# First stage of a two-stage transform: from one 90-frequency product per part to a 60-frequency and a 30-frequency product, with the second stage one step later

## The chip, the cores and the metric

The kernel runs on one core of one Trainium2 chip. The metric is device time in microseconds (us) of one launch; lower is better. Before the change, three runs gave 921.55, 926.01 and 921.55 us, median 921.55 us. The profiled execution took 916.37 us, of which 914.5 us lie between the first and the last instruction (the span). Shares and durations below are of that span.

## The reference

The reference is a long convolution followed by a soft mixture of experts. All is float32.

```python
# x: (8, 5696, 128), h: (5696, 128)
Y = irfft(rfft(x, 2*S, axis=1) * rfft(h, 2*S, axis=0), 2*S, axis=1)[:, :S, :]
# the result, as 45568 tokens of 128 channels, goes through soft MoE
logits = Y @ phi                       # 32 slots
slot_input = softmax_over_tokens(logits).T @ Y
slot_out[e] = relu(slot_input[e] @ w1[e]) @ w2[e]   # 8 experts, 4 slots each
out = softmax_over_slots(logits) @ slot_out
```

## The kernel before

The convolution is a transform, a product of spectra and a transform back. A sequence of 5696 = 89 x 64 tokens is seen as 89 rows of 64 columns, and 5760 = 90 x 64 frequencies are computed: one of each conjugate pair of an 11520-point transform, so that real tables suffice. The work goes in three parts that run at the same time, each some steps behind the one ahead of it.

**Part A, the first stage** (`stage_a`, L205 to L220). It works on chunks: 9 groups (the filter h and the 8 batches) times 8 chunks make 72. A chunk is 4 columns and the 4 mirrored ones, loaded by `load_x` (L179) into one of 3 buffers `xc`, on partitions 20 to 108. `fold` (L196, GpSimd) makes from them the sum (comp 0) and the difference (comp 1), 128 x 512 each, in `x0` and `x1`. `stage_a(c, comp)` then multiplies the folded rows by two of three tables: 90 frequencies, in two runs of 45 that stand at columns F0 = 6 and F1 = 82 of a stationary operand of 128 columns. Each product fills one PSUM bank (128 x 512); ScalarE copies it into `fst`, and two DMAs of 45 rows write the result to an HBM scratch `f` of the group. A chunk thus costs 4 products, 4 evictions and 4 DMAs.

**Part B, the second stage** (`load_g`, `stage_b1`, `stage_b2`, L230 to L302). It works on units: 12 for each group, 11 of 4 pairs of frequencies and a last one of 1. A unit is loaded from `f` (`gt`, 3 buffers, two units ahead), multiplied on TensorE in 64 x 64 pieces (L250), multiplied by the filter's spectrum on VectorE (L268, L277), transformed back by the second stage of the inverse (L292), evicted by ScalarE (L297) and written to a scratch `z`. Since a unit needs all chunks of its group, B runs behind A by LAG_B steps.

**Part C** (`load_pair`, `stage_c1` to `stage_c6`). It works on 32 pairs of chunks, one for every two steps: load from `z` (`zc`), inverse of the first stage (L347), unfolding (VectorE L352, L353, GpSimd L366), transposes (L375), logits (L384), softmax pieces and the slot sums (L460). It runs LAG_C steps behind A.

After the last step a tail finishes C, runs the experts (L762 to L792) and writes the output (L817 to L834).

**What sets the order.** The program order is written out by hand: one loop over steps t (L561), in which each engine's instructions are queued in the order of the calls. Step t holds chunk t of A, 1 or 2 units of B in turn (`PER`), and half of a pair of C. Every engine works through its own queue in that order. Nearly all DMAs are issued by SyncE (SP), also in order: a DMA that has to wait for its data holds up those behind it in SP's queue. The lags are

```python
LAG_B, LAG_C = NJ + 1, 3 * NJ + 3      # 9 and 27 (NJ = 8)
```

A is at two places of a step: `stage_a(t, 0)` and `fold(t + 1, 0)` first (L589), `stage_a(t, 1)` and `fold(t + 1, 1)` late (L630). Between them lie B's first slot, C's products or transposes, B's second slot, and the loads for later steps. `prefetch` (L568) issues a unit's load as soon as its group has been through A by program order (`queue[loaded][0] // NW * NJ + NJ <= t`); the DMA itself waits for the writes of `f`. `bank()` hands out 4 PSUM banks in a ring, which A and C share. `fst` has 5 buffers.

The loop has 81 steps: 9 with A alone, 8 with A and the filter's B, 10 with A and the first batch units, 45 with A, B and C, and 9 with B and C alone.

Of the kernel before, what the change touches and what calls it, by code (L numbers as in the profile page):

```python
# [10 lines left out]
F32 = mybir.dt.float32  # L11
# [8 lines left out]
    return [(0, 64, 32), (64, n - 64, 0)]  # L20


def transform_tables(S, N1, N2, CH, X0, F0, F1):

    N, R1, HALF, P = N1 * N2, S // N2, N2 // 2, 2 * N2
    k1 = np.arange(N1)
    alpha = np.pi * (k1 + 0.5) / N1
    m1 = np.arange(R1) - (N1 - 1) / 2
    a1 = np.outer(m1, alpha)  # L40
    s1 = np.stack([np.cos(a1), -np.sin(a1), -np.cos(a1)], 1)
    a0 = np.outer(alpha, np.arange(N1 // 2) + 0.5)
    i1 = np.stack([np.cos(a0), -np.sin(a0), -np.cos(a0)], 1)
    NP = N1 // 2
    part = s1
    s1 = np.zeros((P, 3, P))
    for a, p in enumerate((F0, F1)):
        s1[X0:X0 + R1, :, p:p + NP] = part[:, :, a * NP:(a + 1) * NP]
    part = i1[np.arange(N1).reshape(2, NP).T.reshape(-1)]
    i1 = np.zeros((P, 3, N2))  # L50
    for r, n, p in z_blocks(N1):
        i1[p:p + n, :, 0:NP] = part[r:r + n]
    k2 = np.arange(N2)
    omega = np.pi * (k1[:, None] + 2 * N1 * k2[None] + 0.5) / N
    m2 = np.arange(HALF) - (N2 - 1) / 2
    a2 = m2[None, :, None] * omega[:, None, :]
    w = np.concatenate([np.cos(a2), np.sin(a2)], 1)
    back = np.arange(N2).reshape(2, HALF // CH, CH).transpose(1, 0, 2).reshape(-1)
# [12 lines left out]
    return [np.ascontiguousarray(t, dtype=np.float32) for t in (s1, i1, wq, vq, tn)]  # L71
# [3 lines left out]
def kernel(  # L75
# [24 lines left out]
    nc = tc.nc  # L100
    P = 128
    B, S, D = x.shape
    NSL = moe_phi.shape[1]
    E, _, F = moe_w1.shape
    SPE = NSL // E
    NFC = F // P
    N1, N2 = 90, 64
    R1, HALF, NP = S // N2, N2 // 2, N1 // 2
    CH = 4
    NJ = HALF // CH  # L110
# [5 lines left out]
    HP = P // 2  # L116
    NQ = NJ // 2
    assert S == R1 * N2 and R1 == N1 - 1 and D == P and CH == Q == 4
    SPLIT = R1 // 16 * 16
    X0, F0, F1 = 20, 6, 82  # L120
    ctx.enter_context(tc.manual_schedule())

    t_s1, t_i1, t_w, t_v, t_turn = [
        nc.inline_tensor(t, f"tab_{n}").ap()
        for n, t in zip(("s1", "i1", "w", "v", "turn"), transform_tables(S, N1, N2, CH, X0, F0, F1))]
    fd = [nc.dram_tensor(f"f_{g}", (2, N2, NP, 2, D), F32, kind="Internal").ap() for g in range(B + 1)]
    zd = [nc.dram_tensor(f"z_{b}", (NP, 2 * N2, 2, D), F32, kind="Internal").ap() for b in range(B)]
    cd = nc.dram_tensor("c_t", (P, B * NQ, Q, 2, MH), F32, kind="Internal").ap()
# [7 lines left out]
    i1 = const.tile([P, 3, HP], F32, name="i1")  # L136
# [21 lines left out]
    apool = lead.enter_context(tc.tile_pool(name="apool", bufs=2, side="right"))  # L158
    bpool = front.enter_context(tc.tile_pool(name="bpool", bufs=1))

    s1 = apool.tile([P, 3, P], F32, name="s1", tag="s1", bufs=1)
    wt = fconst.tile([P, NP, HP], F32, name="wt")
    vt = fconst.tile([P, NU, 2, HP], F32, name="vt")
    turn = fconst.tile([P, 2, NW, 2, 2], F32, name="turn")
# [6 lines left out]


    xs = {}
    xf = [apool.tile([P, CH, D], F32, name=f"x{i}", tag=f"x{i}", bufs=1) for i in range(2)]
    xcs = [apool.tile([P, 2, CH, D], F32, name=f"xc{i}", tag=f"xc{i}", bufs=1) for i in range(3)]
    for t_ in xcs:
        nc.vector.memset(t_[:, :, :, :], 0.0)
# [16 lines left out]
    folded = {}  # L194

    def fold(c, comp):  # L196
        if c not in xs:
            return
        t_ = xs.pop(c) if comp else xs[c]
        y_ = xf[comp]  # L200
        nc.gpsimd.tensor_tensor(out=y_[:, :, :], in0=t_[:, 0, :, :], in1=t_[:, 1, ::-1, :],  # L201
                                op=AL.subtract if comp else AL.add)
        folded[(c, comp)] = y_

    def stage_a(c, comp):  # L205
        g, j = divmod(c, NJ)
        src = folded.pop((c, comp))
        tab = (0, 1) if comp == 0 else (1, 2)
        st = apool.tile([P, CH, 2, D], F32, name="fst", tag="fst", bufs=5)
        for G in range(2):  # L210
            p = bank()
            nc.tensor.matmul(p[:, :], s1[:, tab[G], :],  # L212
                             src[:, :, :].rearrange("p n d -> p (n d)"), start=True, stop=True)
            nc.scalar.activation(st[:, :, G, :],  # L214
                                 p[:, :].rearrange("p (n d) -> p n d", d=D), AF.Copy)
        n0 = comp * HALF + CH * j
        for a, p in enumerate((F0, F1)):
            nc.sync.dma_start(
                out=fd[g][a, n0:n0 + CH, :, :, :].rearrange("n q c d -> q n (c d)"),
                in_=st[p:p + NP, :, :, :].rearrange("k n c d -> k n (c d)"))  # L220


    gs, prods = {}, {}

# [303 lines left out]
        tail["once"] = once  # L528


    LAG_B, LAG_C = NJ + 1, 3 * NJ + 3
    PER = [1, 2] * (NJ // 2)
    assert sum(PER) == NW
    NA, NC = (B + 1) * NJ, B * NJ
# [26 lines left out]
    for t in range(last_front + 1):  # L561
        us = list(units(t))

        def pair(lag):
            T, half = divmod(t - LAG_C - lag, 2)
            return T if half == 0 and 0 <= T < NT else None

        def prefetch(last):  # L568
            nonlocal loaded
            while loaded < len(queue) and queue[loaded][0] <= last \  # L570
                    and queue[loaded][0] // NW * NJ + NJ <= t:
                load_g(queue[loaded][0])
                loaded += 1

        turns = {2: (1, 3), 1: (2,)}.get(len(us), ())

        def slot_b(place=None):
            if place is not None and place not in turns:
                return
            fresh = bool(us)  # L580
            if fresh:
                u = us.pop(0)
                prefetch(u + AHEAD)
                stage_b1(u, t < LAG_C or t >= NA)
                wait_b2.append(u)
            if len(wait_b2) > fresh:
                stage_b2(wait_b2.pop(0))

        if t < NA:  # L589
            stage_a(t, 0)  # L590
            fold(t + 1, 0)
        if pair(3) is not None:
            dispatch(pair(3))
        if t < last_front:
            slot_b(1)
        T, U = pair(0), pair(2)
# [12 lines left out]
        rows = (lambda: None) if U is None else (lambda: stage_c4(U))  # L609
        after = None  # L610
        if T is not None:
            after = stage_c1(T, rows)
        else:
            rows()
        if pair(1) is not None:
            stage_c2(pair(1))
        if pair(5) is not None:
            stage_c6(pair(5))
        if after:
            after()  # L620
        slot_b(2)
        if pair(-2) is not None:
            load_pair(pair(-2))
        if t < NA:
            load_x(t + 3)
        if t == NJ:
            prefetch(AHEAD)
        if U is not None:
            stage_c5(U)
        if t < NA:  # L630
            stage_a(t, 1)
            fold(t + 1, 1)
        if pair(1) is not None:
            stage_c3(pair(1))
        slot_b(3)
        if pair(1) is not None:
            column_max(pair(1))
        if U is not None:
            softmax(U)
        if t == NA:  # L640
            lead.close()
            wts = inner.enter_context(tc.tile_pool(name="wts", bufs=1, side="right"))
            w1s = wts.tile([P, E, F], F32, name="w1s")
        if NA < t <= NA + E:
            nc.sync.dma_start(out=w1s[:, t - NA - 1, :], in_=moe_w1[t - NA - 1])


# [10 lines left out]
                      in_=zring[0][gap, :, :, :, :, :].rearrange("k h o n c d -> k (h o n c d)"))  # L658
# [7 lines left out]
    y_ = tail["pool"].tile([P, Q * CH, D + 1], F32, name="y2", tag="y2", bufs=1)  # L666
# [27 lines left out]
    for V in range(T, NT):  # L694
# [169 lines left out]
```

## Time and profile before

| what | value |
|---|---|
| median time | 921.55 us |
| span of the profile | 914.5 us |
| busy: TensorE, VectorE, ScalarE, GpSimd | 89%, 71%, 53%, 44% |
| bytes moved by DMA, mean rate | 272.43 MB, 298 GB/s |
| time of DMA packets on the SP queue | 91.7% of 16 DMA engines' span |
| first-stage products (L212) | 576 records, 273.9 us |
| first-stage evictions (L214) | 288, 171.8 us |
| folds (L201) | 144, 183.1 us |
| writes of `f` (L218) | 288 DMAs of 180 KB |

A matmul of float32 leaves two records in the profile, so 576 records are 288 products. Busy time of TensorE is that of overlapping, pipelined instructions; the chain of waits (what released what, followed back from the end) tells better how long a product holds up the next one. The share of DMA is the time that packets took on the 16 DMA engines; since packets overlap a little, it can pass 1.00 where the engines always have work.

### The profile page before, as it was taken

What the parts mean: (1) busy time and instruction counts of PE and PEld (TensorE: products, weight loads), DVE (VectorE), ACT (ScalarE), POOL (GpSimd) and SP (SyncE); (2) the same over time, 40 slices, a digit from 0 to 9 for tenths busy, and PEclk for the clock granted to TensorE, in tenths of its full rate; (3) what the DMA queues carried; (4) which work ended last, traced back from release to release, by engine and by line L of the source; (5) the groups of instructions that cost most, each with busy time, mean ns of one, the idle gap of its engine ahead of it and who ended that gap; (6) DMA issues with size and microseconds to landing.
All of it is one profiled execution on the core that took longest, in us unless ns stands there. A gap on an engine that the chain in (4) does not pass through costs nothing.

```text
span 914.5 us, 19226 instructions
## 1 busy us (share of the span) xinstructions
PE 812.2 (89%) x7220; PEld 425.9 (47%) x7220; DVE 645.8 (71%) x928; ACT 481.1 (53%) x888; POOL 405.2 (44%) x385
## 2 busy tenths in 40 slices
PE   6968888799999999999999999999988776978893
PEld 2323344344454444544555445444444443345783
DVE  3058767667888878877888777868888885774552
ACT  4624445456556565655666565555654344474442
POOL 4624333245555555555555555555533432472000
PEclk9989999999999999999999999999999998788865
DMA  9999899999999999999999999989989998751798
GB/s 302 269 282 310 256 326 347 292 323 340 285 324 331 304 281 323 320 329 280 329 323 317 289 317 313 311 281 325 334 266 338 305 295 206 223 220 74 281 404 340
DMA packets 156550, 272.43 MB, mean 298 GB/s; under 512 B 11766, under 2 KB 114422, under 8 KB 153317
## 3 DMA queue, kind: packets, MB, share of 16 engines
q1 hardware_dynamic: 155883, 270.85, 91.7%
q8 instruction: 58, 0.95, 0.4%
q10 hardware_dynamic: 576, 0.36, 0.2%
q14 instruction: 33, 0.27, 0.1%
HBM read 142.86 MB, written 128.21 MB: 296 GB/s over the span
## 4 chain that ended last, share of the span: by engine, by line
PE 61%; DMA 27%; issue 4%; ACT 2%; DVE 2%; POOL 2%; SPq 1%; DVEq 0%; POOLq 0%; ACTq 0%
PE bank L212 19%; PE bank L347 10%; PE bt L250 9%; DMA zc<-z 8%; PE bz L292 7%; DMA gt<-f 6%; DMA out_dram<-o 4%; PE bank L375 3%; PE bank L460 3%; DMA zd<-z 3%; DMA z<-zst 2%; DMA f<-fst 2%; PE bank L384 2%; PE bank L436 2%; PE op L817 1%
## 5 line engine op out<-in xcount | busy, mean ns | idle before, releaser
L201 POOL TENSOR_TENSOR x<-xc 128x512 f32<-128x512 f32 x144 | 183.1, 1273 | 260.5 <-PE bank L212 156.9
L212 PE MATMUL bank<-x,s 128*128 128x512 f32 x576 | 273.9, 611 | 9.7 <-POOL x L201 9.6
L214 ACT ACTIVATE fst<-bank 128x512 f32<-128x512 f32 x288 | 171.8, 597 | 94.7 <-PE bank L212 88.3
L297 ACT ACTIVATE zst<-bz 128x1024 f32<-128x1024 f32 x96 | 93.2, 971 | 195.2 <-PE bz L292 191.5
L268 DVE TENSOR_TENSOR p<-bt,Hi 128x1024 f32<-128x1024 f32 x96 | 113.0, 1177 | 107.3 <-PE bt L250 107.1
L212 PEld LDWEIGHTS bank<-x,s 128*128 128x128 f32 x576 | 102.1, 192 | 126.9 <-issue 94.1
L250 PE MATMUL bt<-gt,wt 64*64 64x256 f32 x1620 | 117.4, 397 | 40.0 <-DMA gt<-f 19.8
L347 PE MATMUL bank<-zc,i 128*64 128x512 f32 x480 | 118.0, 614 | 8.5 <-DMA zc<-z 6.2
L277 DVE TENSOR_TENSOR yf<-bt,p 128x512 f32<-128x512 f32 x192 | 119.4, 663 | 3.3
L268 DVE TENSOR_TENSOR bt<-bt,Hr 128x1024 f32<-128x1024 f32 x96 | 113.0, 1178 | 0.0
L250 PEld LDWEIGHTS bt<-gt,wt 64*64 64x64 f32 x1620 | 55.9, 134 | 117.0 <-issue 61.7
L292 PE MATMUL bz<-yf,vt 64*64 64x256 f32 x1440 | 103.7, 386 | 0.0
L366 POOL TENSOR_TENSOR y<-y,op 128x512 f32<-128x512 f32 x64 | 77.4, 1209 | 11.8 <-DVE op L352 9.1
L292 PEld LDWEIGHTS bz<-yf,vt 64*64 64x64 f32 x1440 | 61.8, 136 | 21.1
L366 POOL TENSOR_TENSOR y<-y,om 128x512 f32<-128x512 f32 x54 | 64.0, 1185 | 2.1
L347 PEld LDWEIGHTS bank<-zc,i 128*64 128x64 f32 x480 | 30.9, 138 | 70.3 <-issue 47.4
L375 PE MATMUL bank<-ident,y 109*128 109x109 f32 x512 | 57.5, 268 | 0.7 <-DVE y L366 0.7
L375 PEld LDWEIGHTS bank<-ident,y 109*128 109x128 f32 x512 | 51.2, 146 | 12.9 <-POOL L L449 6.2
L421 POOL MEMSET dt<- 64x8 f32 x32 | 3.4, 106 | 115.9 <-issue 69.2
L377 ACT ACTIVATE yt<-bank 128x360 f32<-128x360 f32 x128 | 50.2, 483 | 2.1 <-PE bank L375 2.1
L817 PE MATMUL op<-so,cT 32*128 32x128 f32 x704 | 46.2, 369 | 4.3 <-ACT o L826 3.4
L268 DVE TENSOR_TENSOR p<-bt,turn 128x1024 f32<-128x1024 f32 (+1 forms) x12 | 14.1, 1176 | 50.7 <-PE bt L250 50.6
(97 smaller groups left out, 861.5 us busy)
## 6 DMA issues: line engine op xcount, KB each, us to landing
f<-fst SPq DMA_DIRECT2D x288, 180.0 KB
gt<-f SPq DMA_DIRECT2D x99, 512.0 KB
z<-zst SPq DMA_DIRECT2D x88, 512.0 KB
zc<-z SPq DMA_DIRECT2D x30, 1024.0 KB
xc<-in_x_dram SPq DMA_DIRECT2D x64, 320.0 KB
out_dram<-o SPq DMA_DIRECT2D x16, 1024.0 KB
zc<-z SPq DMA_DIRECT2D x30, 416.0 KB
out_dram<-o SPq DMA_DIRECT2D x8, 768.0 KB
```

Source lines behind the costliest of these rows:

```text
L201: nc.gpsimd.tensor_tensor(out=y_[:, :, :], in0=t_[:, 0, :, :], in1=t_[:, 1, ::-1, :], op=AL.subtract if comp else AL.add)
L212: nc.tensor.matmul(p[:, :], s1[:, tab[G], :], src[:, :, :].rearrange("p n d -> p (n d)"), start=True, stop=True)
L214: nc.scalar.activation(st[:, :, G, :], p[:, :].rearrange("p (n d) -> p n d", d=D), AF.Copy)
L250: nc.tensor.matmul(bt[q * HP:(q + 1) * HP, a, o, :], wt[r, 2 * i + q, :], t_[r, 2 * o + q, :, :].rearrange("p c d -> p (c d)"), start=True ...
L268: nc.vector.tensor_tensor(out=p_, in0=pv, in1=h_, op=AL.mult)
L277: eng.tensor_tensor(out=y_[r, 0:k, c, :], in0=pv[:, :, c, :], in1=pi[r, 0:k, 1 - c, :], op=op_)
L292: nc.tensor.matmul(bz[a * HP:(a + 1) * HP, q, o, :], vt[r, i, a, :], y_[r, a * m + o, :, :].rearrange("p c d -> p (c d)"), start=True, sto ...
L297: nc.scalar.activation(st[:, 0:m, 0:n, :].rearrange("p o q x -> p q o x"), bz[:, 0:n, 0:m, :], AF.Copy)
L347: nc.tensor.matmul(p[h_ * HP:(h_ + 1) * HP, :], i1[0:kr, tab, :], t_[0:kr, h_, o, :, q, :], start=True, stop=True)
L366: eng.tensor_tensor(out=part_, in0=part(v, 0), in1=o_[:, :, :], op=sign)
L375: nc.tensor.transpose(p[:, i * TR:(i + 1) * TR], ys[T][0:TR, k * CH + i, 0:D], ident[0:TR, 0:TR])
L817: nc.tensor.matmul(pq[q][:, k * D:(k + 1) * D], cT[rows, b, r0:r0 + RW, :] if k < n else cL[rows, :, :], so4[rows, :], start=True, stop=True)
```

## The change

The 90 frequencies of the first stage are split 60 + 30 in place of 45 + 45. The low 60 take 64 columns of the array, so that the sum and the difference of a chunk stand side by side in one bank (`first_low`, each step). The high 30 take 32 columns, so that four parts, sum and difference of two chunks, stand abreast in one bank (`first_high`, each odd step). The stationary table is cut from 128 to 96 columns for each of its 3 kinds. The folded parts have 4 buffers in place of 2, since a chunk's parts now wait for the next chunk; `fst` has 4 in place of 5. Where C runs, `first_low` stands at the start of a step, and `first_high` of an odd step in the middle, behind the transposes of C, together with both folds for the next step. On even steps both folds stand at the start. The rows of `f` keep their layout, and are written by DMAs of 45, 15 and 30 rows. Each lag grows by one step, so the loop has 82 steps.

```diff
-    for a, p in enumerate((F0, F1)):
-        s1[X0:X0 + R1, :, p:p + NP] = part[:, :, a * NP:(a + 1) * NP]
+    NA = N1 * 2 // 3
+    s1[X0:X0 + R1, :, 0:NA] = part[:, :, 0:NA]
+    s1[X0:X0 + R1, :, N2:N2 + N1 - NA] = part[:, :, NA:N1]
...
-    xf = [apool.tile([P, CH, D], F32, name=f"x{i}", tag=f"x{i}", bufs=1) for i in range(2)]
+    xf = [apool.tile([P, CH, D], F32, name=f"x{i}", tag=f"x{i}", bufs=1) for i in range(4)]
...
-        y_ = xf[comp]
+        y_ = xf[c % 2 * 2 + comp]
...
-    def stage_a(c, comp):
-        tab = (0, 1) if comp == 0 else (1, 2)
-        st = apool.tile([P, CH, 2, D], F32, name="fst", tag="fst", bufs=5)
+    def first_stage(tiles, width):
+        st = apool.tile([P, CH, 2, D], F32, name="fst", tag="fst", bufs=4)
         for G in range(2):
             p = bank()
-            nc.tensor.matmul(p[:, :], s1[:, tab[G], :],
-                             src[:, :, :].rearrange("p n d -> p (n d)"), start=True, stop=True)
+            for o, (c, comp) in enumerate(tiles):
+                k = slice(0, HP) if width == HP else slice(HP, HP + QP)
+                nc.tensor.matmul(p[o * width:(o + 1) * width, :], s1[:, comp + G, k],
+                                 folded[(c, comp)][:, :, :].rearrange("p n d -> p (n d)"),
+                                 start=True, stop=True)
             nc.scalar.activation(st[:, :, G, :],
                                  p[:, :].rearrange("p (n d) -> p n d", d=D), AF.Copy)
...
+        for o, (c, comp) in enumerate(tiles):
+            runs = ((0, 0, 0, NP), (1, 0, NP, N1A - NP)) if width == HP else ((1, N1A - NP, 0, N1 - N1A),)
+            for a, q, p_, n in runs:
+                p_ += o * width
+                nc.sync.dma_start(
+                    out=fd[g][a, n0:n0 + CH, q:q + n, :, :].rearrange("n q c d -> q n (c d)"),
+                    in_=st[p_:p_ + n, :, :, :].rearrange("k n c d -> k n (c d)"))
+
+    def first_low(c):
+        first_stage([(c, comp) for comp in range(2)], HP)
+
+    def first_high(c):
+        both = [(c - 1 + i, comp) for i in range(2) for comp in range(2)]
+        first_stage(both, QP)
...
-    LAG_B, LAG_C = NJ + 1, 3 * NJ + 3
+    LAG_B, LAG_C = NJ + 2, 3 * NJ + 4
...
+        def high(t):
+            if t % 2:
+                first_high(t)
+            fold(t + 1, 0)
+            fold(t + 1, 1)
...
         if t < NA:
-            stage_a(t, 0)
-            fold(t + 1, 0)
+            first_low(t)
+            if t % 2 == 0 or t < LAG_C:
+                high(t)
...
             stage_c6(pair(5))
+        if t < NA and not (t % 2 == 0 or t < LAG_C):
+            high(t)
         if after:
             after()
         slot_b(2)
...
-        if t < NA:
-            stage_a(t, 1)
-            fold(t + 1, 1)
...
-        if NA < t <= NA + E:
+        if NA < t < NA + E:
```

More of the change, by code (lines that the diff above doesn't have):

```diff
@@ L20, in z_blocks, with transform_tables @@
     return [(0, 64, 32), (64, n - 64, 0)]
-def transform_tables(S, N1, N2, CH, X0, F0, F1):
+def transform_tables(S, N1, N2, CH, X0):
     N, R1, HALF, P = N1 * N2, S // N2, N2 // 2, 2 * N2
@@ L45, in transform_tables @@
     part = s1
-    s1 = np.zeros((P, 3, P))
-    for a, p in enumerate((F0, F1)):
-        s1[X0:X0 + R1, :, p:p + NP] = part[:, :, a * NP:(a + 1) * NP]
+    s1 = np.zeros((P, 3, N2 + N2 // 2))
+    NA = N1 * 2 // 3
+    s1[X0:X0 + R1, :, 0:NA] = part[:, :, 0:NA]
+    s1[X0:X0 + R1, :, N2:N2 + N1 - NA] = part[:, :, NA:N1]
     part = i1[np.arange(N1).reshape(2, NP).T.reshape(-1)]
@@ L119 @@
     SPLIT = R1 // 16 * 16
-    X0, F0, F1 = 20, 6, 82
+    X0 = 20
+    QP = HP // 2
+    N1A = N1 * 2 // 3
     ctx.enter_context(tc.manual_schedule())
@@ L124 @@
         nc.inline_tensor(t, f"tab_{n}").ap()
-        for n, t in zip(("s1", "i1", "w", "v", "turn"), transform_tables(S, N1, N2, CH, X0, F0, F1))]
+        for n, t in zip(("s1", "i1", "w", "v", "turn"), transform_tables(S, N1, N2, CH, X0))]
     fd = [nc.dram_tensor(f"f_{g}", (2, N2, NP, 2, D), F32, kind="Internal").ap() for g in range(B + 1)]
@@ L159 @@
     bpool = front.enter_context(tc.tile_pool(name="bpool", bufs=1))
-    s1 = apool.tile([P, 3, P], F32, name="s1", tag="s1", bufs=1)
+    s1 = apool.tile([P, 3, HP + QP], F32, name="s1", tag="s1", bufs=1)
     wt = fconst.tile([P, NP, HP], F32, name="wt")
@@ L203, in fold @@
         folded[(c, comp)] = y_
-    def stage_a(c, comp):
-        g, j = divmod(c, NJ)
-        src = folded.pop((c, comp))
-        tab = (0, 1) if comp == 0 else (1, 2)
-        st = apool.tile([P, CH, 2, D], F32, name="fst", tag="fst", bufs=5)
+    def first_stage(tiles, width):
+        st = apool.tile([P, CH, 2, D], F32, name="fst", tag="fst", bufs=4)
         for G in range(2):
             p = bank()
-            nc.tensor.matmul(p[:, :], s1[:, tab[G], :],
-                             src[:, :, :].rearrange("p n d -> p (n d)"), start=True, stop=True)
+            for o, (c, comp) in enumerate(tiles):
[3 more added lines that the diff above has]
+                                 start=True, stop=True)
             nc.scalar.activation(st[:, :, G, :],
                                  p[:, :].rearrange("p (n d) -> p n d", d=D), AF.Copy)
[L216 to L220, printed above, removed]
+        for o, (c, comp) in enumerate(tiles):
+            g, j = divmod(c, NJ)
+            n0 = comp * HALF + CH * j
+            runs = ((0, 0, 0, NP), (1, 0, NP, N1A - NP)) if width == HP else ((1, N1A - NP, 0, N1 - N1A),)
[9 more added lines that the diff above has]
+        first_stage(both, QP)
+        for b_ in both:
+            del folded[b_]
     gs, prods = {}, {}
```

## The prediction

> **What bounds the kernel now.** I read the page first (busy shares, the DMA row of the 40 slices), then the windows of the stretch in which A, B and C run together, then its chain of waits, then SP's own waits.
>
> ```profile
> PE 812.2 (89%) x7220; PEld 425.9 (47%) x7220; DVE 645.8 (71%) x928; ACT 481.1 (53%) x888; POOL 405.2 (44%) x385
> ...
> DMA  9999899999999999999999999989989998751798
> ...
> L212 PE MATMUL bank<-x,s 128*128 128x512 f32 x576 | 273.9, 611 | 9.7 <-POOL x L201 9.6
> ```
>
> Two resources are near full at once, TensorE and the DMA engines. The windows (busy us of each engine, then clock, DMA share, GB/s) say where:
>
> ```profile
> 225.00:660.00 435.00, 425.73 (x3788) 214.21 (x3790) 347.23 (x499) 260.45 (x478) 237.76 (x220) 1.00 0.98 312
> ...
> 500.00:505.00 5.00, 5.00 (x40) 2.99 (x42) 2.82 (x4) 4.29 (x9) 1.93 (x2) 1.00 0.93 263
> 505.00:510.00 5.00, 5.00 (x31) 1.88 (x25) 4.31 (x9) 3.03 (x5) 1.59 (x2) 1.00 0.61 185
> 510.00:515.00 5.00, 3.99 (x34) 1.87 (x33) 3.86 (x6) 1.82 (x5) 2.89 (x4) 1.00 0.95 294
> 515.00:520.00 5.00, 4.87 (x44) 2.40 (x42) 4.38 (x8) 3.64 (x7) 4.46 (x5) 1.00 1.06 333
> ```
>
> In the middle TensorE is busy 98%, and DMA 0.98. DMA dips at a group's end, and TensorE idles right after it. One pair of steps in the chain of waits is all TensorE:
>
> ```profile
> 269.66 1.87 PE bank L347 x8
> ...
> 274.00 3.44 PE bank L212 x8
> 277.44 1.02 PE bank L460 x32
> 278.47 1.02 PE bt L250 x16
> 279.49 0.86 PE bz L292 x16
> ...
> 282.45 1.81 PE bank L212 x4
> 284.27 0.74 PE bank L384 x8
> 285.01 1.02 PE bt L250 x16
> 286.04 0.86 PE bz L292 x16
> 286.90 1.91 PE bank L212 x4
> ```
>
> From 269.66 to 291.27, where L347 comes again, are 21.6 us, of which L212 holds 7.16. Between the L347 pieces at 248.51 and 665.12 the chain has 19 pairs, 21.93 us each: some 0.35 us a pair are not TensorE's. SP's own waits name the dip:
>
> ```profile
> SPq L236 <- DMA f<-fst: 40.1, 9, 8.3
> ...
> SPq L328 <- DMA z<-zst: 28.9, 12, 4.4
> ```
>
> At each group's end the load of the next `gt` stands in SP's queue until the last write of `f` has landed, 4.5 us on average, and nothing behind it is issued.
>
> [...] the 128*64 products of L347 take 1.87 us for four, 0.93 for two side by side; the 128*32 products of L762 take 3.64 us for 16, 0.91 for four abreast. [...] the 15-row DMAs could be slower in themselves; no row of before shows such a transfer.
>
> **The change part by part.**
>
> *Products.* Removed per pair of steps: 8 products, 7.16 us in the chain. Added: two low stages (two pairs of 64 columns each), 2 x 1.87 = 3.74, by L347; one high stage (two fours of 32 columns), 2 x 0.91 = 1.82, by L762. Sum 5.56, so -1.6. TensorE's pair becomes 21.58 - 1.6 = 20.0 us. Bounds: 0.81 for a four (L384's, of only 360 columns, in the timeline) to 1.0 (an estimate, a tenth above L762's) give 5.4 to 5.7.
>
> *Folds.* The fold of t+1 behind `first_high` of an odd step cannot start before those products end, as they read the same buffers. Two folds take 2 x 1.27 = 2.55 us (L201). Queued on TensorE in that time: L384 0.74, L250 1.02, L292 0.86 = 2.62. It just covers; for the semaphores I add 0.1. Pair: 20.1. On even steps the folds stand a step ahead. Their cost on GpSimd is hidden (44% busy), and two more buffers cost nothing in time.
>
> *Evictions.* 6 in place of 8 per pair, -1.2 us on ScalarE (0.597 each), which is not the bound: worth nothing.
>
> *DMA bytes.* Unchanged. Per pair, from the issues of the page: `f` 1440 KB, `x` 712, `gt` 1440, `z` 1440, `zc` 1440, `c_t` 180 = 6652 KB, 6.81 MB. The 5 us windows from 470 to 560 with a share of 1.00 or more move 339 GB/s on average, so a pair needs 20.1 us of full DMA. Dips add: at this group's end (0.93, 0.61, 0.95, and 0.85 at 525) some 3 us in four pairs, 0.75 a pair. DMA's pair before was 20.85.
>
> *DMA issues.* 12 writes of `f` a pair in place of 8, at 0.32 to 0.73 us on SP (minimum, and mean in the middle): +1.3 to 2.9 us. SP issues 315 us of 435 in the middle, 15.9 us a pair[...]; 17 to 19 of 20.8 still fits. I take it as hidden.
>
> *The lag of B.* The last chunk of a group is now through A a step and a half ahead of the first load of its unit (the condition of `prefetch` and the new lag), some 13 us, more than the landing of a write (8.8 us at its longest in the chain). The stall of 40.1 us on SP goes, the one before `zc` stays, so half the dips: DMA's pair becomes 20.1 + 0.3 = 20.4.
>
> *The pair after.* Before, the larger of TensorE (21.58) and DMA (20.85) was passed by 0.35. After: 20.4 + 0.4 = 20.8 us.
>
> *One more step.* A and B and C run together for 44 steps in place of 45, A alone for 10 in place of 9, B and C alone for 10 in place of 9. A step of A alone is about 4.4 us (chain from 20 to 43). A step of B and C is 9.5 us: L347 comes at 698.86, 718.52 and 736.95 (9.2 to 9.8), where VectorE, not A, is full. But the stall ahead of the first `gt` (43.64 to 52.40 in the chain, a write and a load, 8.7 us) loses its write, -4.
>
> Sum: middle 22 x 20.8 - 22.5 x 21.93 = 457.6 - 493.4 = -35.8; A alone +4.4 - 4; A and B, which is DMA's already (0.97 from 103 to 190), two dips less, -3; B and C +9.3. Total -29 us: 921.55 - 29 = 892.
>
> **The rivals.**
>
> *TensorE stays the bound alone.* DMA keeps up without dips, a pair takes 20.1: 22 x 20.1 - 493.4 = -51.2, +6.7 for the rest: -44.5, 877 us. For it: windows of 370 GB/s exist. Against: they follow dips, and are catching up.
>
> *DMA is the wall already.* Packets took 0.98 of the engines' time in the middle[...]. Pair 21.6: 475.2 - 493.4 = -18.2, +6.7: -11.5, 910 us. For it: `zc` waits of 10 to 13 us in the chain. Against: shares of 1.03 go with 339 GB/s, above the mean of 312.
>
> *A new wait on the folds or in SP's queue.* TensorE waits for the whole fold at every second step (x arrives late: GpSimd waited 60.8 us for it in the middle; or SP, with 4 more issues, falls behind). Pair 20.1 + 2.6 = 22.7: 499.4 - 493.4 = +6, +6.7: 934 us, slower. For it: the cover is 0.1 us thin, and SP is in order. Against: the load of x has half a step more time than before.
>
> **How the numbers follow.** Chances: 892 at 0.56, 877 at 0.12, 910 at 0.18, 934 at 0.14. The range goes from 874, just below TensorE's bound (the low end of a four), to 914, a little above DMA's wall, and leaves out the new wait. Slower by over 0.5%: 0.12; within 0.5% (917 to 926): 0.04, the edges of the last two; faster 0.84.
>
> **What would show it.** Low stages of 1.87 us and high ones of 1.8 in the chain of waits; pairs of 20.8 us by L347's successor; SP's wait for `f` near zero, that for `z` as before; DMA at 0.98 or more and 320 GB/s or more in the middle; 288 + 144 writes of `f`, with the same time of packets. I am wrong if folds release the low products for more than 0.5 us a pair, if the DMA rate stays at 312, or if the steps of B and C at the end grow.

## The result

The changed kernel took 980.57 us (median of 4 runs, 971.09 to 984.19), the kernel before 923.78 us beside it. The ratio is 1.060, 95% interval 1.051 to 1.068: 6% slower, where I had forecast 892 us.

The first lines of the page of the changed kernel, its first-stage products, and the stretch from 225 to 660 us in the same columns as before:

```profile
PE 789.7 (81%) x7796; PEld 399.1 (41%) x7796; DVE 625.8 (65%) x928; ACT 438.2 (45%) x816; POOL 404.4 (42%) x385
...
L215 PE MATMUL bank<-x,s 128*32 128x512 f32 (+1 forms) x1152 | 239.3, 625 | 20.2 <-POOL x L204 19.1
...
DMA 46%; PE 33%; SPq 7%; issue 4%; DVE 4%; ACT 2%; POOL 1%; ACTq 0%; POOLq 0%; DVEq 0%
```

```profile
225.00:660.00 435.00, 381.05 (x3836) 188.81 (x3828) 306.34 (x466) 222.46 (x409) 224.38 (x208) 0.98 0.96 292
```

TensorE is busy 381 of 435 us in place of 426, in part because fewer pairs of steps fall into the stretch (some 18.7 in place of 19.9, by the table below), but the work does not come closer together: the chain that ended last is 46% DMA and 33% TensorE. The DMA engines move 292 GB/s where they had moved 312, at nearly the same share of time. The chain of waits shows the products as forecast, a low stage and a high stage, and between them what now sets the pace:

```profile
260.89 1.87 PE bank L215 x8
...
456.39 1.85 PE bank L215 x16
...
549.47 9.90 DMA zc<-z
...
594.43 10.92 DMA zc<-z
...
617.40 10.15 DMA zc<-z
```

TensorE's idle time says the same. Ahead of the products that read `zc` it grew from 8.5 to 46.3 us, nearly all of it a wait for `zc` (the kernel before, then the changed one):

```profile
L347 PE MATMUL bank<-zc,i 128*64 128x512 f32 x480 | 118.0, 614 | 8.5 <-DMA zc<-z 6.2
...
L364 PE MATMUL bank<-zc,i 128*64 128x512 f32 x480 | 122.9, 635 | 46.3 <-DMA zc<-z 44.2
```

SyncE's own waits changed too. The wait of the `gt` load (L253) for the last write of `f`, 40.1 us before, is not in the list any more, as forecast. At the top stands a wait of the same load for `zc`, with which it shares no data. That wait is not new, and by itself it is no measure of the loss: it was 51.8 us before, and is 61.0 us in the kernel with the lag alone (e2 below), the fastest of all. The three, and two more waits of the changed kernel (us in total, times, longest):

```profile
SPq L236 <- DMA zc<-z: 51.8, 15, 4.7
...
SPq L236 <- DMA zc<-z: 61.0, 17, 5.3
...
SPq L253 <- DMA zc<-z: 70.6, 21, 5.3
...
SPq L317 <- DMA zc<-z: 27.1, 19, 2.7
SPq L345 <- DMA z<-zst: 23.5, 15, 4.0
```

Where the time went can be read from one eviction that comes once in every pair of C, `om` on ScalarE, in the timeline: when it first runs (A and B have filled the pipeline), how long the next 22 pairs take, and what is left. The table has the profiled execution of each kernel, in us; single executions of a kernel differ by 1% and more, so the verdicts below go by the timed runs.

| kernel | first `om` | next 22 pairs | rest | span |
|---|---|---|---|---|
| before | 186.1 | 480.1 | 248.3 | 914.5 |
| changed | 213.2 | 511.6 | 244.5 | 969.3 |
| lag alone (e2) | 188.1 | 469.0 | 250.0 | 907.1 |
| writes cut alone (e1) | 193.7 | 521.5 | 254.4 | 969.5 |
| changed, 8 writes a pair (e3) | 200.7 | 483.6 | 250.6 | 934.9 |
| the same, halves in turn (e5) | 197.4 | 475.2 | 244.1 | 916.7 |
| changed, x ahead of zc (e17) | 214.7 | 490.5 | 247.8 | 953.0 |

Of the 54.8 us between the two spans, 27.1 are lost ahead of C's first `om` and 31.5 in the 22 pairs; the end is 3.8 us shorter. A pair takes 23.25 us (511.6 / 22), where I had 20.8.

### The profile page after: what moved, and what is told of

Its sections match the earlier page's. It is cut to its first block, busy times and chain, and to the rows that moved or that the text cites. A ratio compares the mean times of both kernels' runs of the same rounds, so it can differ in the third digit from the quotient of the medians.

```text
span 969.3 us, 20414 instructions
## 1 busy us (share of the span) xinstructions
PE 789.7 (81%) x7796; PEld 399.1 (41%) x7796; DVE 625.8 (65%) x928; ACT 438.2 (45%) x816; POOL 404.4 (42%) x385
## 3 DMA queue, kind: packets, MB, share of 16 engines
q1 hardware_dynamic: 158043, 270.86, 89.8%
## 4 chain that ended last, share of the span: by engine, by line
DMA 46%; PE 33%; SPq 7%; issue 4%; DVE 4%; ACT 2%; POOL 1%; ACTq 0%; POOLq 0%; DVEq 0%
DMA zc<-z 22%; PE bank L364 11%; DMA z<-zst 9%; PE bank L215 7%; SPq L226 5%; PE bt L267 5%; DMA gt<-f 4%; DMA out_dram<-o 3%; PE bz L309 3%; DMA zd<-z 2%; PE bank L430 1%; PE op L840 1%; DMA f<-fst 1%; DMA xc<-in_x_dram 1%; PE bank L392 1%
## 5 line engine op out<-in xcount | busy, mean ns | idle before, releaser
L204 POOL TENSOR_TENSOR x<-xc 128x512 f32<-128x512 f32 x144 | 179.8, 1271 | 338.1 <-PE bank L215 205.3
L215 PE MATMUL bank<-x,s 128*32 128x512 f32 (+1 forms) x1152 | 239.3, 625 | 20.2 <-POOL x L204 19.1
L218 ACT ACTIVATE fst<-bank 128x512 f32<-128x512 f32 x216 | 127.5, 597 | 126.7 <-PE bank L215 100.5
L267 PE MATMUL bt<-gt,wt 64*64 64x256 f32 x1620 | 120.0, 407 | 68.5 <-DMA gt<-f 29.7
L364 PE MATMUL bank<-zc,i 128*64 128x512 f32 x480 | 122.9, 635 | 46.3 <-DMA zc<-z 44.2
L215 PEld LDWEIGHTS bank<-x,s 128*32 128x32 f32 (+1 forms) x1152 | 65.2, 128 | 143.3 <-issue 68.9
L267 PEld LDWEIGHTS bt<-gt,wt 64*64 64x64 f32 x1620 | 58.6, 138 | 143.8 <-issue 87.7
L309 PE MATMUL bz<-yf,vt 64*64 64x256 f32 x1440 | 105.8, 390 | 0.0
L309 PEld LDWEIGHTS bz<-yf,vt 64*64 64x64 f32 x1440 | 64.2, 138 | 20.3 <-issue 0.6
L383 POOL TENSOR_TENSOR y<-y,om 128x512 f32<-128x512 f32 x54 | 64.1, 1187 | 2.1
L369 DVE TENSOR_TENSOR y<-bank,y 128x512 f32<-128x512 f32 x32 | 22.1, 690 | 63.4 <-PE bank L364 63.4
L285 DVE TENSOR_TENSOR p<-bt,turn 128x1024 f32<-128x1024 f32 (+1 forms) x12 | 14.1, 1176 | 70.9 <-PE bt L267 70.9
```

The source lines that it names most:

```text
L215: nc.tensor.matmul(p[o * width:(o + 1) * width, :], s1[:, comp + G, k], folded[(c, comp)][:, :, :].rearrange("p n d -> p (n d)"), start=Tr ...
L218: nc.scalar.activation(st[:, :, G, :], p[:, :].rearrange("p (n d) -> p n d", d=D), AF.Copy)
L267: nc.tensor.matmul(bt[q * HP:(q + 1) * HP, a, o, :], wt[r, 2 * i + q, :], t_[r, 2 * o + q, :, :].rearrange("p c d -> p (c d)"), start=True ...
L285: nc.vector.tensor_tensor(out=p_, in0=pv, in1=h_, op=AL.mult)
L309: nc.tensor.matmul(bz[a * HP:(a + 1) * HP, q, o, :], vt[r, i, a, :], y_[r, a * m + o, :, :].rearrange("p c d -> p (c d)"), start=True, sto ...
L364: nc.tensor.matmul(p[h_ * HP:(h_ + 1) * HP, :], i1[0:kr, tab, :], t_[0:kr, h_, o, :, q, :], start=True, stop=True)
```

## The experiments

My theory after the result was that the smaller and more numerous writes of `f` cost the time (W). Its rivals were the order of products and folds (O) and the later second stage (L).

### The parts one by one

**e1: the kernel before with the changed kernel's writes.**

```diff
-        for a, p in enumerate((F0, F1)):
+        for a, q, p, n in ((0, 0, F0, NP), (1, 0, F1, 15), (1, 15, F1 + 15, 30)):
             nc.sync.dma_start(
-                out=fd[g][a, n0:n0 + CH, :, :, :].rearrange("n q c d -> q n (c d)"),
-                in_=st[p:p + NP, :, :, :].rearrange("k n c d -> k n (c d)"))
+                out=fd[g][a, n0:n0 + CH, q:q + n, :, :].rearrange("n q c d -> q n (c d)"),
+                in_=st[p:p + n, :, :, :].rearrange("k n c d -> k n (c d)"))
```

> The kernel before, with one edit: the second 45-row write of f of each part is cut into 15 and 30 rows, so that a pair of steps has the changed kernel's 12 writes and their sizes; products, order, partitions and lags are those of before. Theory W (the smaller and more numerous writes of f slow the DMA engines or SyncE's queue, and that is the loss): 940 to 980 us. Theory O (the loss comes from the order, low products bunched ahead and folds behind the high ones): within 1% of 922 us. Theory L (the later second stage costs it): within 1% of 922 us.

Measured: 970.3 us, ratio 1.047 (1.039 to 1.056). Cutting one write in two, with nothing else changed, costs 44 us by the ratio (0.0473 x 922).

**e2: the lag alone.**

```diff
-    LAG_B, LAG_C = NJ + 1, 3 * NJ + 3
+    LAG_B, LAG_C = NJ + 2, 3 * NJ + 4
...
-        if NA < t <= NA + E:
+        if NA < t < NA + E:
```

> The kernel before, with both lags one step longer and nothing else. My prediction's own sum for this part: the stall of SyncE on f at a group's end goes (some 2 to 7 us won), one step more of A alone and of B and C alone (13 us lost), so 920 to 932 us, with the wait of SyncE for f near zero. Theory L: 950 us or more. Theories W and O: below 935 us.

Measured: 911.14 us, ratio 0.982 (0.976 to 0.988): faster than the kernel before, and better than my own sum for this part. L falls. The middle of it is TensorE's alone:

```profile
225.00:660.00 435.00, 434.12 (x3856) 216.23 (x3854) 355.92 (x514) 266.78 (x489) 237.03 (x221) 1.00 1.00 321
```

TensorE is busy 434 of 435 us, and a pair takes 21.36 us (mean of 19), within what the chain of before had for TensorE's own work, 21.2 to 21.6. SyncE's wait of `gt` for `f`, 40.1 us before, is not in its list. The longer lag also moves C by one step against the even and odd steps of A; no run separates that from the stall.

**e3: the changed kernel with the old writes.**

```diff
-            runs = ((0, 0, 0, NP), (1, 0, NP, N1A - NP)) if width == HP else ((1, N1A - NP, 0, N1 - N1A),)
+            runs = ((0, 0, 0, NP), (1, 0, N1A - NP, NP)) if width == HP else ()
```

> The changed kernel, but its low stage writes two runs of 45 rows for each part (rows 0 to 44 and 15 to 59 of the 60) and its high stage writes nothing: 8 writes of 180 KB in a pair of steps as in the kernel before, the same bytes, products, evictions and order as the changed kernel. The 30 high frequencies are left out of f, so the convolution lacks them. Theory W: 885 to 915 us, as the prediction had it. Theory O or L: above 955 us. In between, both.

Measured: 940.43 us, ratio 1.013 (1.007 to 1.019). In between: about 40 us of the loss is the writes (980.6 to 940.4), but without them the kernel is still slower than e2, by 29 us, though TensorE has less to do. Its quickest pairs take 20.2 us, near what I had worked out for TensorE, but this does not show TensorE's own time: in the one from 527.21 to 547.43 us, 10.5 us of the chain are a write of `z` and a load of `zc`. The mean is 21.98 (483.6 / 22).

**e12: lag and cut together.** The edits of e2 and of e1.

> e2_lag_alone (kernel before with both lags one step longer, 911 us), with the second write of each part cut into 15 and 30 rows as in e1_split_writes. If the cost of the writes and the gain of the lag add up: 911 + 40 = 945 to 960 us. If the longer lag makes room for the writes: 930 us or less. If the writes cost more where SyncE no longer stands still: 965 us or more.

Measured: 972.49 us, ratio 1.046 (1.036 to 1.055). The last case: with the writes cut, the gain of the lag is not seen at all. The two do not add up. Part of it can be read from SyncE's waits of e1: with the writes cut, the wait of `gt` for `f`, which the lag removes, is 11.3 us already, in place of 40.1.

### What a write costs

**e7: the second write cut by columns**, so that each half keeps its 45 rows.

```diff
-        for a, p in enumerate((F0, F1)):
+        for a, p, h_, n in ((0, F0, 0, CH), (1, F1, 0, CH // 2), (1, F1, CH // 2, CH // 2)):
             nc.sync.dma_start(
-                out=fd[g][a, n0:n0 + CH, :, :, :].rearrange("n q c d -> q n (c d)"),
-                in_=st[p:p + NP, :, :, :].rearrange("k n c d -> k n (c d)"))
+                out=fd[g][a, n0 + h_:n0 + h_ + n, :, :, :].rearrange("n q c d -> q n (c d)"),
+                in_=st[p:p + NP, h_:h_ + n, :, :].rearrange("k n c d -> k n (c d)"))
```

> The kernel before, with the second write of f of each part cut in two by columns: 2 x (45 rows x 2 KB) in place of 45 rows x 4 KB, so 12 writes a pair of steps as in e1_split_writes, but every one from 45 rows. Theory N (the number of writes costs, by SyncE or by what each takes on the DMA engines): 960 to 980 us, as e1_split_writes (970). Theory P [...]: 920 to 935 us.

Measured: 975.92 us, ratio 1.049 (1.027 to 1.071), as e1, though with a wide interval. The number of writes counts, not how few partitions one has: 1.047 with pieces of 15 and 30 rows (e1), 1.049 with two of 45 rows. Theory P stands here for writes of 15 and 30 rows being slow in themselves, which I had named as a risk with no trace to show it; this run shows no part of the loss there.

**e9 and e10: a small write more.** Behind each part's two writes, one more to a scratch: of 1 row of 512 bytes (e9), or of 15 (e10).

```diff
+        nc.sync.dma_start(out=sd[2 * c + comp, 0:1, :], in_=st[F0:F0 + 1, 0, 0, :])
```

> The kernel before, with one more write behind the two of each part: one row of 512 bytes to a scratch that nobody reads, so 4 more DMAs in a pair of steps and next to no bytes. Theory S (what costs is the issue of a DMA in SyncE's queue, whatever it moves): 955 to 980 us, as with the writes cut in two. Theory E (what costs is what a write does on all the DMA engines [...]): 920 to 935 us.

> As e9_tiny_writes, but each added write has 15 rows of 512 bytes[...]; 30 KB more in a pair of steps, 0.5% of its bytes. Theory S: the same as e9_tiny_writes, 955 to 980 us. Theory E: clearly above e9_tiny_writes, 945 us or more, with e9 near 925.

Measured: e9 965.95 us, ratio 1.042 (1.036 to 1.048); e10 982.09 us, 1.061 (1.053 to 1.068). 144 writes that move 74 KB in all cost 39 us, almost as much as cutting the real ones (44 us, e1). So it is SyncE's queue, in some way. Spreading the small write over 15 rows costs a further 16 us (982.09 - 965.95). Such a write also holds SyncE longer, 0.72 us in the mean of the stretch from 225 to 660 us where that of one row takes 0.41, so whether the DMA engines have a part in the 16 us is not shown. SyncE's waits of e9 name `zc` again, now ahead of the writes:

```profile
SPq L219 <- DMA zc<-z: 71.5, 18, 5.5
SPq L222 <- DMA zc<-z: 37.0, 21, 3.7
```

L222 is the small write. It needs nothing that `zc` brings, and waits 37 us for it.

### Why SyncE waits for zc

The traces of the kernel before and of the changed one show what a DMA of SyncE's queue waits for, beside its data. Of the 764 DMAs of the kernel before that have another eight places ahead in the queue, all 764 start after that one has landed; in the changed kernel it is all 908. So at most eight are in flight, by number and not by size: the queue holds loads of x of 36 KB and loads of `zc` of 1024 KB alike. This is also what ends most of SyncE's pauses. From 225 to 660 us the kernel before has 73 pauses over 0.3 us, 144.3 us in all, and 57 of them, 84.5 us, end 16 to 82 ns after the DMA eight places ahead has landed. In the changed kernel these are 73 of 83 pauses, 114.4 of 131.2 us.

The two loads of `zc` together are 1440 KB and take 9.6 and 11.1 us to land (medians of the kernel before, 225 to 660 us); whoever stands eight places behind them holds up the whole queue until then (`gt` in the kernel before: the 51.8 us in 15 waits above). A small write uses up a place and brings the next DMA one place nearer to `zc`. Two theories were left: places, or the issue time that SyncE spends on each DMA.

**e13 and e14: the same four small writes, behind zc or ahead of it**, once in a pair, in `load_pair`.

```diff
     def load_pair(T):
...
+        for i in range(4):                      # e14: here
+            nc.sync.dma_start(out=sd[T, i:i + 1, :], in_=ident[0:1, :])
         for r, n, p in z_blocks(N1):
             nc.sync.dma_start(out=t_[p:p + n, ...], in_=zd[b]...)
+        for i in range(4):                      # e13: here
+            nc.sync.dma_start(out=sd[T, i:i + 1, :], in_=ident[0:1, :])
         zs[T] = t_
```

> The kernel before, with four writes of one row of 512 bytes to a scratch issued right behind the two loads of zc, once in a pair of steps. [...] with four small writes between, the second write of f, four places nearer to zc, has to wait for zc's 1 MB. Theory of places (a small write costs because it takes one of eight places, and those behind a slow load run out): 960 us or more. Theory of issue time (each DMA costs SyncE the same, wherever it stands): the same as e14_tiny_ahead_of_zc.

> As e13_tiny_behind_zc, with the four small writes right ahead of the two loads of zc: the same number of DMAs and bytes, but what stands behind zc is as in the kernel before. Theory of places: 925 to 945 us, at least 15 us below e13_tiny_behind_zc. Theory of issue time: the same as e13_tiny_behind_zc, 955 to 965 us.

Measured: e13 980.91 us, ratio 1.058 (1.052 to 1.065); e14 925.74 us, 1.000 (0.997 to 1.002). The same DMAs, in the same number, cost 54 us behind `zc` and nothing ahead of it. As an account of these 54 us, the theory of issue time falls, since e14 has the same issues. SyncE's timeline of e13 shows the hole: `zc` at 438.80, four small writes, two loads of x, and then nothing until 449.39, though two writes of `f` at 431.82 took 0.79 us to issue. (By this count it is the first write of `f`, not the second as I wrote, that stands eight places behind the first load of `zc`.)

```profile
438.80 1.86 SPq L329 DMA_DIRECT2D zc<-z  x2
440.72 1.16 SPq L334 DMA_DIRECT2D s_t<-ident  x4
441.98 1.04 SPq L191 DMA_DIRECT2D xc<-in_x_dram  x2
449.39 3.64 SPq L219 DMA_DIRECT2D f<-fst  x4
```

In all of e13, SyncE's writes of `f` wait 121.6 us for `zc` in 44 places; in e14 they do so once, for 1.1 us.

**e17 and e18: zc two places later in the queue.** The loads of x for a later step change places with those of `zc`, in the changed kernel (e17) and in e2 (e18).

```diff
+        if t < NA:
+            load_x(t + 3)
         if pair(-2) is not None:
             load_pair(pair(-2))
-        if t < NA:
-            load_x(t + 3)
```

> The changed kernel, with the two loads of x for a later step issued ahead of the two loads of zc in place of behind them, and nothing else. Eight places behind the first zc load then stands the write of c_t in place of the load of gt; gt and z are no longer held up by zc, with the same number of DMAs. Theory of places: 940 to 965 us (980 before the swap), with SyncE's wait of gt for zc (70.6 us) gone or small. If the number of DMAs alone counts: 975 to 985 us.

> e2_lag_alone (kernel before, lags one step longer, 911 us), with the same swap of the loads of x and zc. There TensorE sets the pace of a pair (21.2 to 21.6 us), so that SyncE's waits cost nothing in the middle: 905 to 913 us, and the best version if below e2_lag_alone. If the swap lets zc come later than its use: above 915 us.

Measured: e17 964.07 us, ratio 1.041 (1.032 to 1.049), against 1.060 (1.051 to 1.068) of the changed kernel: some 17 us won by an exchange that leaves the number of DMAs as it is, and all of it in the pairs (490.5 us for 22 in place of 511.6). The wait of `gt` for `zc` is gone; what stands eight places behind now, `c_t` and high writes, waits in its place:

```profile
SPq L512 <- DMA zc<-z: 49.8, 20, 4.1
SPq L226 <- DMA zc<-z: 33.9, 26, 3.1
```

The swap also brings x earlier: from 225 to 660 us GpSimd waits 77.9 us for it in the changed kernel, and no such wait is listed for e17. But TensorE waits for folds some 2 us there in both, so the gain is not that; its wait for `zc` falls from 34.1 to 24.6 us.

e18: 914.04 us, ratio 0.984 (0.975 to 0.993), no different from e2, as expected where TensorE sets the pace (busy 432 of 435 us). e2 stays the version to use.

**The changed kernel itself.** Here the place behind `zc` is not the whole account. `gt` and `z` stand eight and nine places behind it in the kernel before, in e2, in e3 and in the changed kernel alike. From 225 to 660 us they wait 64.4 and 25.3 us for it in the changed kernel, and 64.1 and 23.8 us in e3, which is 40 us faster. What sets them apart is how much of a pair SyncE has left. I split SyncE's time in the traces from 225 to 660 us: the time of its DMA instructions, the pauses that end as the DMA eight places ahead lands ("place"), other pauses over 0.3 us (mostly waits for data), and the short ones between instructions. In us of one pair:

| kernel | pair | issuing | place | data | short |
|---|---|---|---|---|---|
| before | 22.0 | 13.2 | 4.3 | 3.0 | 1.5 |
| e14 | 22.5 | 14.1 | 4.9 | 2.1 | 1.5 |
| lag alone (e2) | 21.3 | 12.8 | 5.3 | 1.9 | 1.4 |
| e3 | 22.0 | 13.9 | 5.6 | 1.1 | 1.4 |
| changed | 23.4 | 14.8 | 6.2 | 0.9 | 1.5 |
| e13 | 24.8 | 14.8 | 7.1 | 1.3 | 1.6 |

In the kernel before, SyncE waits 3.0 us a pair for data, and the issues of e14 come out of that. In the changed kernel 0.9 us are left: issuing and places fill the pair, `zc` is issued late, and TensorE waits for it. The DMA engines run dry at another point, too (means over 17 to 18 pairs). From 12 to 14 us behind the issue of `zc` their share of time is 0.62 in e1, 0.53 in e9 and 0.69 in e13, where the queue has stood still behind `zc`. In the changed kernel it is 0.98 there, and 0.87 to 0.89 from 16 to 20 us, while SyncE issues one DMA after another with hardly a pause. How much of the 40 us over e3 is issuing and how much is places, no run separates.

### Other queues

**e4: the 15-row and 30-row writes from ScalarE's queue; e16: the 15-row writes from GpSimd's.**

```diff
-                nc.sync.dma_start(
+                (nc.sync if n == NP else nc.scalar).dma_start(      # e4
+                (nc.gpsimd if n == 15 else nc.sync).dma_start(      # e16
```

> The changed kernel, with its 15-row and 30-row writes of f issued from ScalarE's queue, so that SyncE issues 4 writes of f a pair of steps in place of 12. Theory W in its form that SyncE's queue is the bound (issue time and order): below 940 us. Theory W in its form that the DMA engines are slower on such writes: 965 to 985 us. Theory O: 965 to 985 us.

> The changed kernel, with its 15-row writes of f issued from GpSimd's queue[...]: SyncE's queue then has 21 DMAs in a pair of steps, as the kernel before. Theory of places: 925 to 950 us. If GpSimd is held up by the issues or by waiting for the evictions: 970 us or more, which tells nothing of the theory. If the DMA engines themselves pay for each write: 970 to 985 us.

Measured: e4 1022.73 us, ratio 1.100 (1.090 to 1.110), worse than any case I had. SyncE's loads of x and `zc` now wait for writes of `f`, with which they share no data:

```profile
SPq L193 <- DMA f<-fst: 127.0, 44, 9.3
SPq L345 <- DMA f<-fst: 83.6, 20, 9.3
```

L193 loads x, and waits 0.2 us for writes of `f` in the changed kernel; L345 loads `zc`, and has no such wait there. Whether the writes are ScalarE's or those left to SyncE is not shown. e16: 983.6 us, ratio 1.060 (1.053 to 1.066). GpSimd stood 183.4 us waiting for evictions ahead of its issues, and the first `om` came at 238.5 us. By what I had written this tells nothing of the theory, though the 22 pairs, 490.2 us in place of 511.6, go its way: what was won there was lost ahead of C.

### What else the changed kernel loses

e3 has the old number of writes, less work for TensorE and the longer lag, and is 29 us slower than e2. Four runs took it apart. All leave the 30 high frequencies out of `f`, as e3.

**e5: the four writes of a step in another order**: parts in turn within each run of rows, so that writes from partitions below 64 and above alternate, as in the kernel before.

```diff
-        for o, (c, comp) in enumerate(tiles):
-            for a, q, p_, n in runs:
+        for a, q, p_, n in runs:
+            for o in [o for i in range(m) for o in (i, i + m)]:
```

> The run with the old 8 writes (e3_old_writes: changed kernel, low stage writes 2 x 45 rows a part, high stage nothing, the 30 high frequencies left out), with the four writes of a step in another order: those from partitions below 64 and those from above take turns, in place of two from below and then two from above. Theory P (neighbouring writes from one half of the partitions slow each other): 905 to 925 us, pairs of steps of 21.2 us or less. Theory O2 (order on TensorE and GpSimd is what e3_old_writes has left): 935 to 945 us, as it.

Measured: 926.89 us, ratio 0.999 (0.995 to 1.003), against 1.013 (1.007 to 1.019) of e3: some 13 us. The 22 pairs take 475.2 us in place of 483.6, and the middle moves 316 GB/s in place of 309. e5 falls short of the 905 to 925 us that I expected of this theory, so it is a part only. The order of the destinations in `f` changes with that of the partitions; no run tells which of the two it is.

**e6: the same order in the changed kernel.**

> The changed kernel, with its writes of f in the order in which the halves of the partitions take turns (45, 45, 15, 15 of the low stage; high stage 1, 3, 2, 4); nothing else. Theory P: 30 us or more below the changed kernel, under 950 us. Theory that the number of writes counts, not their partitions: 970 to 985 us, as the changed kernel.

Measured: 975.48 us, ratio 1.056 (1.041 to 1.072): no difference that can be told, as long as the number of writes is what counts.

**e8: six buffers for the folded parts, in e3. e11: five buffers for fst, in e5. e15: the high stage late in the step from B's start on, in e5.**

```diff
-    ... name=f"x{i}", tag=f"x{i}", bufs=1) for i in range(4)]
+    ... name=f"x{i}", tag=f"x{i}", bufs=1) for i in range(6)]      # e8
-        y_ = xf[c % 2 * 2 + comp]
+        y_ = xf[c % 3 * 2 + comp]                                  # e8
-        st = apool.tile([P, CH, 2, D], F32, name="fst", tag="fst", bufs=4)
+        st = apool.tile([P, CH, 2, D], F32, name="fst", tag="fst", bufs=5)   # e11
-            if t % 2 == 0 or t < LAG_C:
+            if t % 2 == 0 or t < LAG_B:                            # e15, and its counterpart
```

> e3_old_writes with 6 buffers for the folded parts in place of 4 (a chunk's folds no longer wait for the high products of the chunk before; the 30 high frequencies left out of f as there). Theory O2 (folds behind the high products hold up the low ones, mostly while A runs alone): 915 to 930 us. Theory P, or any in which the DMA engines set the pace: 933 to 943 us.

> e5_old_writes_alternate (changed kernel with 8 writes a pair in alternating order; the 30 high frequencies left out of f), with 5 buffers for fst as in the kernel before, in place of 4. Theory F (with 4 buffers the evictions wait for writes while A runs alone or with the filter): about 910 to 917 us, and C's first product some 9 us earlier. Otherwise as e5_old_writes_alternate, 920 to 930 us.

> e5_old_writes_alternate (changed kernel with 8 writes a pair, the 30 high frequencies left out of f), with the high stage of odd steps in the middle of the step from the first step of B on, in place of from the first step of C on. If what e5_old_writes_alternate has left over e2_lag_alone (927 to 911 us) lies in the low and high products that stand together at the start of those steps: 911 to 920 us. If not: 924 to 932 us.

Measured: e8 943.88 us, ratio 1.022 (1.010 to 1.034), no better than e3; e11 930.25 us, 1.002 (0.999 to 1.005), no better than e5; e15 924.29 us, 0.993 (0.988 to 0.998), at most a little better than e5. So neither two more buffers for the folded parts nor one more for the evictions helps. What is left between e5 and e2, some 16 us by the timed runs, is in the profiled executions 9.3 us ahead of C's first `om` (197.4 us in e5, 188.1 in e2) and 6.2 us in the 22 pairs, with an end that is 5.9 us shorter. Ahead of C the traces name the folds: TensorE waits for them 18.5 us in e5 (8.1 of it at the very start), 2.8 us in e2 (without its start, 8.2 us, which is put down to the load of h). It is 16.8 us in e8 (8.0 at the start), so more buffers hardly shorten that wait. The cause of the 6.2 us stays open.

## Why the prediction was wrong

**The lag** was right in its mechanism, and worth more than I gave it. The stall of SyncE on `f` went (40.1 us before, not listed after), and e2 alone gains 1.8% where I had put the longer ramp and end against it. The wait ahead of `zc`, which I had as staying, did not grow: `z` before `zc` 23.5 us after, 28.9 before.

**The products** were right: 1.87 us for a low stage and 1.85 for a high one, 5.59 us a pair in place of 7.16. That a whole pair of TensorE's then takes the 20.1 us that I worked out is not shown, since none of the kernels with these products is held by TensorE alone; the 1.6 us are worth nothing where TensorE is not the last. The 0.1 us in it for the semaphores of two folds fits the trace of the kernel before: of 27 first-stage products and weight loads that wait for a fold, 20 start 51 to 54 ns after its end.

**DMA issues** is the step that failed. I priced four more writes by SyncE's issue time ("+1.3 to 2.9 us ... 17 to 19 of 20.8 still fits. I take it as hidden"). With 25 DMAs in a pair of steps in place of 21, the issuing did grow as priced, by 1.6 us a pair, from 13.2 to 14.8. (I had 15.9 before, from 315 us in the middle; the DMA instructions there add up to 262 us, and a write of `f` takes 0.62 us in the mean, not 0.73.) What I put at nothing is the rest of SyncE's time. A DMA takes one of eight places in flight, the two loads of `zc` hold theirs for some 10 us, and SyncE waited 4.3 us a pair for places before the change and 6.2 after it. With 14.8 us of issuing, 0.9 of waits for data and 1.5 of short pauses these fill the 23.4 us of the pair, so there was nothing left to hide the writes in. That a small DMA costs by its place is shown by e13 and e14 (54 us and nothing), that the number of writes costs by e1, e7 and e9 (ratios of 1.047, 1.049 and 1.042). A view that could have told me was there: SyncE's waits of the kernel before have L236 (`gt`) waiting 51.8 us for `zc` in 15 places, although `gt` needs only `f`. I passed over it and read the line below it.

**The rate of the DMA engines** failed with it. I took 339 GB/s from windows with a share of 1.00 as what a pair could have. The changed kernel has a share of 0.96 and moves 292; e9, with hardly a byte more than before, has 0.94 and 290. My windows were also the fast ones: from 8 to 10 us behind each issue of `zc`, the kernel before has a share of 0.99 as well, and moves 208 GB/s (mean of 19 pairs). A high share is no measure of what the engines could do at their best. A share passes 1.00 since more than 16 packets are under way at times, up to 23 in both kernels from 225 to 660 us. That the cut writes would leave the time of packets as it was, was an estimate of mine. On the SP queue as a whole it grew, from 839 to 870 us of the 16 engines' time (91.7% of 914.5 and 89.8% of 969.3); the writes of `f` are not shown apart.

**The ramp** I had nearly even (+4.4 - 4 - 3). It lost 27.1 us. By the first `om`: the lag alone adds 2.0, the cut writes alone 7.6, the new products and their order (e3 over e2) 12.6, and the three together make 22.2 of the 27.1. They do not simply add: lag and cut in one kernel (e12) add 17.0. The folds, which I had as just covered, are a part of it: ahead of the first `om`, TensorE waits for them 19.1 us (8.1 at the very start), 9.6 before (7.9 at the start). The end, where I had 9.3 us more for a further step of B and C, is 3.8 us shorter.

**The rivals.** The one on the slow side came nearest: a pair of 22.7 us there, 23.25 measured. It named SyncE with four more issues next to the folds, at 0.14, but its number was that of the folds, and its 934 us kept my even ramp, so that the pair came out near is luck. Where A, B and C run together the folds are not it: from 225 to 660 us TensorE waits for them some 2 us in all.

## What to carry to other kernels

Before cutting a transfer in two, look at what SyncE's queue waits for, beside its data. Here a wait for a transfer that shared no data was a place in flight running out (51.8 us of `gt` for `zc` before the change, 70.6 after). It need not cost anything, as e2 shows (61.0 us in the fastest kernel); but where SyncE had little left of waits for data (0.9 us a pair in the changed kernel), more DMAs cost time, and small ones cost about as much as large ones (39 us in e9, 44 in e1). Order can help: let what stands eight places behind a slow load be something that is late anyway (some 17 us in e17). And parts of a change are worth trying alone: the lag, which looked like its price, is what gains 1.8%.

## What I had not expected of the hardware and the program

- Four DMAs of 512 bytes in a pair of steps cost 54 us (1.058) right behind a slow load, and nothing (1.000) right ahead of it.
- The same small write costs 39 us with one row and 55 us with 15 rows (e9, e10); SyncE takes 0.41 and 0.72 us in the mean to issue it.
- Issuing the 15-row and 30-row writes from ScalarE cost 42 us more (e4 over the changed kernel): SyncE's loads of x, which share no data with the writes of `f`, wait 127.0 us for them, where they wait 0.2 us in the changed kernel. What ScalarE's own issuing takes from its evictions is not shown apart.
- Writes that alternate between the lower and the upper half of the partitions were some 13 us faster than two from one half after two from the other (e5 over e3), at the same bytes; the order of their destinations changed with it, and in the changed kernel (e6) the order made no difference that can be told.
